# Gathered expert slots in batches of eight instead of four, and a ring of fourteen row buffers instead of twelve

## The chip, the cores and the metric

The kernel runs on one core of one Trainium2 chip. Five engines work on their own instruction streams and wait for each other by semaphores: TensorE (PE; its weight loads are PEld), VectorE (DVE), ScalarE (ACT), GpSimd (POOL) and SyncE (SP), which here only issues transfers. The metric is the time of one execution on the device in microseconds; lower is better. Where several runs are given, the median counts.

## What is computed

One layer: the input, plus attention with 32 heads of 16 columns that share one key and one value head, plus a product-key mixture of experts. 2048 tokens of 512 columns, all in fp32:

```python
xn = layernorm(x)
# A: q = xn @ wq (32 heads of 16), one k and v for all heads, softmax, @ wo
# B: for each token and each of 32 query heads
s1, s2 = q1 @ k1.T, q2 @ k2.T            # 64 scores each
i1, i2 = the two best of each            # four candidates, the two best of them: top_s, top_e
g = softmax(top_s)
act = gelu(xn . u[top_e])                # u, v: 4096 rows of 512 columns
out = sum over 32 heads x 2 of g * act * v[top_e]
return x + A(xn) + B(xn)
```

The kernel takes the 32 query heads in 8 chunks c of four. So each token has 64 expert rows: 8 chunks, four heads, two rows each.

## The kernel before

The 16 tiles of 128 tokens form four groups of four. The whole program is one long, hand-ordered stream: a start stage (layer norm, keys, values, queries), then 256 attention steps. A step is one unit of attention for one block of 128 keys: four score matmuls `sc` (L412), two exponentials `pt` on ACT (L419), sixteen matmuls `pv` (L429). Between them `fill()` lets PE do other work up to a planned time: the query-key products of the expert search (`psc`, L631) with their top-two search on DVE (L644, L646), and later the dense experts.

The experts run in two ways. For groups 0 and 1 (`NSP = 2`) each token's expert row is **gathered**. `slots` lists 512 of them: 2 groups, 8 chunks, 2 pairs of tiles, four heads, two rows a head, two tiles. A slot `m` passes through four functions, each with a counter of its own:

- `gather(m)` (L1084): POOL issues an indirect transfer (L1091) that fetches, for 128 tokens, one row of 1024 fp32 columns (u and v side by side) into a tile `g`. These tiles come from a ring of `NGB` buffers; a buffer may be written again when its last reader has run. `gathers(most)` (L1145) issues a gather only while fewer than `NGB - lent` slots lie between the next gather and the next add.
- `dot(m)` (L1096): DVE multiplies u with the normed token tile and sums (L1103, one custom operation and a read of its accumulator) into one column of a tile `act` of `SB` columns. With the last column of a batch, three small operations of `SB` columns are put on the list `CHAIN`: `gq` (L1112), `gy` (L1113) for gelu's polynomial, and `ga` (L1114), activation times gate. The gates of a chunk lie in a tile `gg` of tokens x 4 tiles x 4 heads x 2.
- `tanhs(to)` (L1162): ACT takes one tanh a batch (L1119) and marks the batch ready (`a_ready`). `weigh(n)` makes the batch's weights on DVE (L1126).
- `add(m)` (L1129): DVE adds weight times v to the tile's sum (L1138), a `scalar_tensor_tensor` of 128x512. This is the last reader of the ring buffer. The sum lies in a tile `xa`, which has the normed tokens beside it.

Groups 2 and 3 are **dense**: the gates of all tokens are spread into one-hot products (`oh` on DVE, L892 to L895; `pg` on PE, L925; the *gate stage*, `dense_on == 2`), and then 32 blocks of experts run as full matmuls `pact` (L833) and `pout` (L971), with `gy`, `wd`, `wk` and `da` on DVE in between (the *dense stage*; `wk` splits a loaded block `rw` in two parts, `gy` is the activation, `wd` the split of it).

The main loop sets the order of slots: in each step `pos` grows by a rate for the stage (1.0 dot a step in a gate stage, 1.5 in a dense stage, 1.75 to 2.6 else), and `mid()` emits, in this order, tanhs of complete batches, the step's dots but one, `weigh`, the last dot, and then `go()`: it takes adds, chain operations and operations of the other work (`rest`: `wk`, `gy`, `wd`) in turn, and at its end up to four gathers. The number of adds is at most the number of dots or three, whichever is more, and at most two once `dense_on` is 3 or 4. In a gate stage the chain runs at once, ahead of the one-hots, and `go()` later.

Three times the ring gives two of its buffers to the output weights `wo` (`lent = 2`, L484), until a block of four tiles is done. A finished tile is stored by SP (`experts_out`, L540 and L543), and the four tiles `xa` of the second group reuse the buffers of the first (`load_phase2_tile`, L1195, with the transfers L1197 and L1198), called with the first gather of each. SP issues its transfers strictly in order. `rc` (L467) is a reciprocal for the softmax sums of attention.

The lines of the batch size and the ring, as the kernel has them:

```python
SB = 4
NGB = 12
# in add(): the weight of a batch, made when its first add needs it
weigh(n)
if i == SB - 1:
    weigh(n + 1)
# in gathers():
while g_next[0] < NSL and g_next[0] < a_next[0] + NGB - lent[0] and most > 0:
# in tanhs():
while a_ready[0] + SB <= to:
    tanh(a_ready[0] // SB)
    a_ready[0] += SB
```

Of the kernel before, what the change touches and what calls it, by code (L numbers as in the profile page):

```python
# [12 lines left out]
F16 = mybir.dt.float16  # L13
# [10 lines left out]
P = 128  # L24
# [12 lines left out]
NSP = 2  # L37
NB = 32
NEG = 8
SB = 4  # L40
NGB = 12
NWK = 8
NIDX = 9
GS = 8192.0
# [14 lines left out]
def tile_kernel(ctx, tc, x, wq, wkv, wo, wqT, kT, uv, ub, vb, out):  # L59
# [3 lines left out]
    const = pool("const", bufs=1)  # L63
# [4 lines left out]
    start = start_stack.enter_context(tc.tile_pool(name="start", bufs=1))  # L68
# [44 lines left out]
    for j in range(4):  # L113
        v = blk_f[:, 8 * j:8 * j + 8]
# [4 lines left out]
    nc.gpsimd.tensor_copy(blk, blk_f)  # L119
    iota_i = start.tile([P, P], I32, name="iota_i")  # L120
    nc.gpsimd.iota(iota_i, pattern=[[1, P]], base=0, channel_multiplier=0)
    iota_h = const.tile([P, P], F16, name="iota_h")
    nc.gpsimd.tensor_copy(iota_h, iota_i)

    gtile = lambda dt=F32, shape=(P, 1024), name="g": big.tile(list(shape), dt, name=name, tag="g", bufs=NGB)
    xtile = lambda name: ps.tile([P, 512], F32, name=name, tag="x", bufs=3)
# [357 lines left out]
    def load_wo():  # L484
        WO.clear()
        for h in range(2):
            if lent[0]:
                assert g_next[0] - a_next[0] <= NGB - 2
                w = gtile(F32, (P, 2, D), "wo")
# [161 lines left out]
    IDX, G = {}, {}  # L651
# [432 lines left out]
    def gather(m):  # L1084
        ph, c, ti, s = slots[m]
        if s == 0:
            run_scores(key=(ph, c, ti))
            if ph and c == 0:
                load_phase2_tile(TPH * ph + ti)
        gt = gtile()  # L1090
        nc.gpsimd.indirect_dma_start(  # L1091
            out=gt, out_offset=None, in_=uv,
            in_offset=bass.IndirectOffsetOnAxis(ap=IDX[ph, c, ti][:, s:s + 1], axis=0))
        UV[m] = gt

    def dot(m):  # L1096
        ph, c, ti, s = slots[m]
        n, i = divmod(m, SB)
        if i == 0:
            ACTS[n] = small.tile([P, SB], F32, name="act", bufs=3)  # L1100
        a = ACTS[n]
        u = UV[m][:, :D]
        nc.vector.tensor_tensor_reduce(u, u, XN[TPH * ph + ti], scale=1.0, scalar=0.0,  # L1103
                                       op0=OP.mult, op1=OP.add, accum_out=a[:, i:i + 1])
        if i == SB - 1:
            q = small.tile([P, SB], F32, name="gq", bufs=3)
            y = small.tile([P, SB], F32, name="gy", bufs=3)
            ga = small.tile([P, SB], F32, name="ga", bufs=4)
            gg = G[ph, c][:, ti - 1:ti + 1, s // 2, :].rearrange("p t k -> p k t")
            pairs = lambda v: v.rearrange("p (k t) -> p k t", t=2)  # L1110
            stt = nc.vector.scalar_tensor_tensor
            CHAIN.append(lambda: stt(q, a, C_CUB, a, op0=OP.mult, op1=OP.mult))  # L1112
            CHAIN.append(lambda: stt(y, q, C_IN, a, op0=OP.add, op1=OP.mult))  # L1113
            CHAIN.append(lambda: nc.vector.tensor_tensor(out=pairs(ga), in0=pairs(a), in1=gg, op=OP.mult))  # L1114
            TH[n], GA[n] = y, ga
# [29 lines left out]
    def gathers(most):  # L1145
        while g_next[0] < NSL and g_next[0] < a_next[0] + NGB - lent[0] and most > 0:
            gather(g_next[0])
            g_next[0] += 1
            most -= 1

    def dots(to):
        while d_next[0] < min(to, NSL):
            dot(d_next[0])
            d_next[0] += 1
# [18 lines left out]
    def run(fns):  # L1173
        todo = fns[:]
        fns.clear()
        for fn in todo:
            fn()
# [144 lines left out]
    with tc.manual_schedule(engines=ENGINES):  # L1322
# [80 lines left out]
        load_q(0)  # L1403
        gathers(NGB // 2)
        transpose_group(3)
# [32 lines left out]
    with tc.manual_schedule(engines=ENGINES):  # L1438
# [80 lines left out]
        while a_next[0] < NSL:  # L1519
# [4 lines left out]
            run(STORES)  # L1524
            gathers(NGB)
        assert not OUTS
# [3 lines left out]
def build(nc, tc, args):  # L1530
    tile_kernel(tc, *args)
# [33 lines left out]
```

## Time and profile before

| what | value |
|---|---|
| three runs | 1822.09, 1819.43, 1818.98 us; median 1819.43 |
| the profiled execution | 1823.24 us, of which its span is 1821.5 us |
| granted TensorE clock, mean | 0.998 |
| busy, share of the span | PE 96%, DVE 89%, ACT 71%, POOL 38% |
| the chain that ended last | PE 48%, DVE 32%, DMA 6%, issue 4%, ACT 3% |

A busy microsecond is one in which the engine had an instruction under way; overlapping ones are counted once. The chain that ended last is followed back from the last instruction, at each step to what released it. In a row of the groups stand the line, the engine, the operation with the names it writes and reads, the shapes and the count; then busy microseconds in all and the mean of one in ns; then the idle time of the engine just ahead of these instructions, and who ended it. In a timeline stand start, length and the instruction, and in brackets the idle time ahead of it.

### The profile page before, as it was taken

The numbers are of one execution on the slowest core, as the hardware profiler recorded it, in microseconds if no ns is written. First come the engines' busy times: TensorE is split into PE (matmuls) and PEld (weight loads), VectorE is DVE, ScalarE is ACT, GpSimd is POOL, SyncE is SP. The second block draws the span as 40 slices with busy tenths as digits, with TensorE's granted clock in tenths as the row PEclk, the third lists the DMA queues.
The fourth block names the chain that finished last, engine by engine and source line by source line (L and its number), as shares of the span: only waits on it lengthen the run. The fifth ranks groups of instructions, "written<-read, shape, count | busy, mean of one in ns | idle before, by whom it ended". The sixth has DMA issues, their size and how long they took to land.

```text
span 1821.5 us, 34944 instructions
## 1 busy us (share of the span) xinstructions
PE 1743.2 (96%) x10997; PEld 880.0 (48%) x10997; DVE 1625.8 (89%) x6385; ACT 1290.0 (71%) x1750; POOL 698.9 (38%) x922
## 2 busy tenths in 40 slices
PE   7999999999998889999999999999988899999998
PEld 4644444555554334555555444555543344555553
DVE  7749989999899977999999798999989778999994
ACT  5367766656568987888787565556689877888874
POOL 1124544435442122444444353345521124444440
PEclk9999999999999999999999999999999999999999
DMA  8489897996764777988899987877636768898883
GB/s 287 175 303 376 303 339 248 347 336 237 242 201 132 238 243 223 284 276 290 283 313 325 321 311 240 291 249 249 229 98 232 251 189 292 286 308 286 286 283 105
DMA packets 243705, 478.31 MB, mean 263 GB/s; under 512 B 93748, under 2 KB 117316, under 8 KB 243516
## 3 DMA queue, kind: packets, MB, share of 16 engines
q0 software_dynamic: 73728, 268.47, 43.6%
q1 hardware_dynamic: 169372, 206.93, 34.2%
q8 instruction: 87, 1.43, 0.3%
q14 instruction: 102, 0.84, 0.1%
q10 hardware_dynamic: 416, 0.66, 0.1%
HBM read 419.94 MB, written 51.15 MB: 259 GB/s over the span
## 4 chain that ended last, share of the span: by engine, by line
PE 48%; DVE 32%; DMA 6%; issue 4%; ACT 3%; POOL 1%; SPq 1%; DVEq 0%; ACTq 0%; POOLq 0%
PE psc L631 16%; PE pv L429 13%; PE sc L412 8%; DVE xa L1138 7%; DVE g L1103 6%; PE pact L833 3%; DVE oh L892 3%; PE pout L971 3%; DVE i L646 2%; DVE da L974 2%; PE pwo L527 2%; ACT pt L419 2%; DVE wk L798 1%; PE pw L583 1%; DMA rsb<-dinv 1%
## 5 line engine op out<-in xcount | busy, mean ns | idle before, releaser
L419 ACT ACTIVATE pt<-sc 128x1024 f32<-128x1024 f32 x1024 | 995.9, 1030 | 379.5 <-PE sc L412 317.8
L1091 POOL DMA_INDIRECT g<-in_uv_dram,idx x512 | 561.0, 1096 | 894.7 <-DVE xa L1138 410.7
L429 PE MATMUL pv<-pt,vaug 128*32 128x512 f32 x4096 | 494.2, 600 | 0.0
L631 PE MATMUL psc<-wk,xt 128*128 128x512 f32 x1536 | 392.8, 403 | 6.9 <-DVE i L646 1.9
L1138 DVE SCALAR_TENSOR_TENSOR xa<-g,w,xa 128x512 f32<-128x512 f32 x512 | 373.5, 748 | 0.1
L412 PE MATMUL sc<-qa,kaug 64*128 64x512 f16 x2048 | 319.6, 382 | 27.6 <-ACT pt L419 22.5
L1103 DVE CUSTOM_DVE_ANT_0 g<-g,xa 128x512 f32<-128x512 f32 x512 | 336.3, 686 | 6.0 <-DMA g<-in_uv_dram,idx 5.9
L631 PEld LDWEIGHTS psc<-wk,xt 128*128 128x128 f32 x1536 | 277.2, 188 | 112.1 <-issue 42.2
L412 PEld LDWEIGHTS <-kaug 64*128 64x128 f16 x2048 | 82.4, 94 | 346.2 <-issue 341.3
L429 PEld LDWEIGHTS pv<-pt,vaug 128*32 128x32 f32 x4096 | 107.0, 109 | 254.9 <-issue 254.9
L646 DVE FIND_INDEX8 i<-m,psc 128x8 uint32<-128x64 f32 x1024 | 207.2, 227 | 0.0
L971 PE MATMUL pout<-wk,wd 128*128 128x512 f32 x768 | 195.2, 401 | 2.7 <-DVE gy L1014 1.5
L833 PE MATMUL pact<-xt,wk 128*128 128x512 f32 x768 | 196.8, 401 | 0.6 <-DVE da L974 0.6
L971 PEld LDWEIGHTS pout<-wk,wd 128*128 128x128 f32 x768 | 140.6, 188 | 49.5 <-issue 5.6
L833 PEld LDWEIGHTS pact<-xt,wk 128*128 128x128 f32 x768 | 139.3, 188 | 49.6 <-issue 18.7
L644 DVE MAX8 m<-psc 128x8 f32<-128x64 f32 x1024 | 146.5, 218 | 10.5 <-PE psc L631 10.1
L798 DVE TENSOR_TENSOR wk<-rw,wk 128x512 fp32r<-128x512 f32 x128 | 85.6, 688 | 8.1 <-ACT wk L797 8.1
L974 DVE TENSOR_TENSOR da<-da,pout 128x512 f32<-128x512 f32 x128 | 82.8, 685 | 6.2 <-PE pout L971 6.2
L892 DVE TENSOR_TENSOR oh<-oh 128x2048 f16<-128x2048 f16 x64 | 78.1, 1220 | 3.3 <-issue 1.9
L646 DVE MATCH_VALUE_LOAD i<-m,psc 128x8 f32 x1024 | 77.7, 76 | 0.0
L797 ACT CAST wk<-rw 128x512 fp32r<-128x512 f32 x128 | 74.4, 636 | 0.0
L690 POOL CAST fi<-i 128x64 f32<-128x64 uint32 x32 | 9.0, 281 | 136.7 <-DVE i L646 131.8
(179 smaller groups left out, 1341.9 us busy)
## 6 DMA issues: line engine op xcount, KB each, us to landing
wk<-dw SPq DMA_DIRECT2D x96, 512.0 KB
wqt<-in_wqT_dram SPq DMA_DIRECT2D x32, 512.0 KB
dw<-wk SPq DMA_DIRECT2D x32, 512.0 KB
rw<-in_ub_dram SPq DMA_DIRECT2D x64, 256.0 KB
rw<-in_vb_dram SPq DMA_DIRECT2D x64, 256.0 KB
gy<-dg SPq DMA_DIRECT2D x64, 256.0 KB
dg<-gst SPq DMA_DIRECT2D x14, 928.0 KB
g<-in_uv_dram,idx POOLq DMA_INDIRECT x512
```

The costliest lines, as they stand in the source:

```text
L412: nc.tensor.matmul(p[:, b, :], kaug[o:o + 64, kc * P:(kc + 1) * P], QA[u][o:o + 64, i, :], start=True, stop=True)
L419: nc.scalar.activation(PT[u, kc, i], p, AF.Exp, scale=SCALE)
L429: nc.tensor.matmul(PV[u][32 * j:32 * j + 32, :], vaug[:, kc, :], pt[:, b, :], start=kc == 0, stop=kc == 15)
L631: nc.tensor.matmul(p, XT[k][:, a, j * P:(j + 1) * P], WC[n_][k][:, bb, :], start=n == 0, stop=n == 11)
L644: nc.vector.max(m8[:, jb, s, :], p[:, s * E:(s + 1) * E])
L646: nc.vector.max_index(i8[:, jb, s, :], m8[:, jb, s, :], p[:, s * E:(s + 1) * E])
L833: nc.tensor.matmul(p, us[:, a, k * P:(k + 1) * P], XT[k][:, c, :], start=n == 0, stop=n == 11)
L892: nc.vector.tensor_tensor(out=oa, in0=num(P), in1=bc(0, tb, P), op=OP.is_equal)
L971: nc.tensor.matmul(p, wd[0][:, a, j * P:(j + 1) * P], vs[:, c, :], start=n == 0, stop=n == 5)
L1091: nc.gpsimd.indirect_dma_start(out=gt, out_offset=None, in_=uv, in_offset=bass.IndirectOffsetOnAxis(ap=IDX[ph, c, ti][:, s:s + 1], axis=0))
L1103: nc.vector.tensor_tensor_reduce(u, u, XN[TPH * ph + ti], scale=1.0, scalar=0.0, op0=OP.mult, op1=OP.add, accum_out=a[:, i:i + 1])
L1138: nc.vector.scalar_tensor_tensor(acc, v, w[:, i:i + 1], acc, op0=OP.mult, op1=OP.add)
```

## The change

`SB` goes from 4 to 8, so a batch is two heads of a pair of tiles, and there are 64 batches instead of 128. `NGB` goes from 12 to 14. To make room for the larger ring the constant `iota_h` moves to the pool that is given back after the start. The view of the gates in `dot` spans two heads instead of one.

```diff
--- before.py
+++ after.py
@@ -37,8 +37,8 @@
 NSP = 2
 NB = 32
 NEG = 8
-SB = 4
-NGB = 12
+SB = 8
+NGB = 14
 NWK = 8
 NIDX = 9
 GS = 8192.0
@@ -119,7 +119,7 @@
     nc.gpsimd.tensor_copy(blk, blk_f)
     iota_i = start.tile([P, P], I32, name="iota_i")
     nc.gpsimd.iota(iota_i, pattern=[[1, P]], base=0, channel_multiplier=0)
-    iota_h = const.tile([P, P], F16, name="iota_h")
+    iota_h = start.tile([P, P], F16, name="iota_h")
     nc.gpsimd.tensor_copy(iota_h, iota_i)
 
     gtile = lambda dt=F32, shape=(P, 1024), name="g": big.tile(list(shape), dt, name=name, tag="g", bufs=NGB)
@@ -1106,8 +1106,9 @@
             q = small.tile([P, SB], F32, name="gq", bufs=3)
             y = small.tile([P, SB], F32, name="gy", bufs=3)
             ga = small.tile([P, SB], F32, name="ga", bufs=4)
-            gg = G[ph, c][:, ti - 1:ti + 1, s // 2, :].rearrange("p t k -> p k t")
-            pairs = lambda v: v.rearrange("p (k t) -> p k t", t=2)
+            h = s // 2
+            gg = G[ph, c][:, ti - 1:ti + 1, h - 1:h + 1, :].rearrange("p t h k -> p h k t")
+            pairs = lambda v: v.rearrange("p (h k t) -> p h k t", h=2, t=2)
             stt = nc.vector.scalar_tensor_tensor
             CHAIN.append(lambda: stt(q, a, C_CUB, a, op0=OP.mult, op1=OP.mult))
             CHAIN.append(lambda: stt(y, q, C_IN, a, op0=OP.add, op1=OP.mult))
```

The instructions of PE are the same 7007 in both programs, in the same order. DVE has 3387 rows before and 3090 now (a row is one instruction as the program names it), ACT 945 and 860, POOL 419 in both, SP 842 and 840. The dots of each step are the same. The gather of a slot stands one step ahead of its dot for 33 of the 512 slots now, and for 6 before.

The first place is DVE in the first dense stage, step 121 to 122. `g` is a ring buffer (the number tells the slot's tile), `xa` a sum or a normed tile, `w` the weight of a batch, `rw`, `wk`, `gy`, `pact` belong to the dense work. Before, the last rows ahead of the dot of slot 246 (the dot of `g_11762` follows as the next row; the add that frees its buffer stands 37 rows ahead of it):

```order
L1138 SCALAR_TENSOR_TENSOR xa_162<-g_11528,w_11908,xa_162 128x512
L1112 SCALAR_TENSOR_TENSOR gq_11905<-act_11829 128x4
L798 TENSOR_TENSOR wk_11899<-rw_11722,wk_11899 128x512
L1138 SCALAR_TENSOR_TENSOR xa_164<-g_11530,w_11908,xa_164 128x512
L1113 SCALAR_TENSOR_TENSOR gy_11906<-gq_11905,act_11829 128x4
L798 TENSOR_TENSOR wk_11901<-rw_11722,wk_11901 128x512
L1138 SCALAR_TENSOR_TENSOR xa_162<-g_11532,w_11908,xa_162 128x512
L1114 TENSOR_TENSOR ga_11907<-act_11829,gg_4460 128x4
L1039 SCALAR_TENSOR_TENSOR gy_11725<-gy_11725,pact_11860 128x512
L1014 SCALAR_TENSOR_TENSOR gy_11725<-gy_11725,pact_11860 128x512
L1103 ISA g_11760,act_11910<-g_11760,xa_168 128x512
L1103 ISA act_11910 128x1
```

Now, from the add of slot 232 (`g_11066`), whose buffer slot 246 takes, to the dot of slot 246 (`g_11575`):

```order
L1139 SCALAR_TENSOR_TENSOR xa_162<-g_11066,w_11567,xa_162 128x512
L798 TENSOR_TENSOR wk_11561<-rw_11394,wk_11561 128x512
L1139 SCALAR_TENSOR_TENSOR xa_164<-g_11128,w_11567,xa_164 128x512
L798 TENSOR_TENSOR wk_11563<-rw_11394,wk_11563 128x512
L1139 SCALAR_TENSOR_TENSOR xa_162<-g_11130,w_11567,xa_162 128x512
L1039 SCALAR_TENSOR_TENSOR gy_11397<-gy_11397,pact_11522 128x512
L1014 SCALAR_TENSOR_TENSOR gy_11397<-gy_11397,pact_11522 128x512
L1103 ISA g_11427,act_11494<-g_11427,xa_168 128x512
L1103 ISA act_11494 128x1
L1103 ISA g_11575,act_11494<-g_11575,xa_166 128x512
```

The three chain operations are gone from this piece, and the add that frees the buffer has moved to nine rows ahead of the dot that needs it.

The second place is DVE in the second dense stage, around slot 405. Before, the first add frees the buffer, and the dot of slot 405 (`g_19536`) follows as the next row:

```order
L1138 SCALAR_TENSOR_TENSOR xa_12166<-g_19113,w_19453,xa_12166 128x512
L798 TENSOR_TENSOR wk_19523<-rw_19339,wk_19523 128x512
L1138 SCALAR_TENSOR_TENSOR xa_12161<-g_19161,w_19529,xa_12161 128x512
L798 TENSOR_TENSOR wk_19525<-rw_19339,wk_19525 128x512
L1138 SCALAR_TENSOR_TENSOR xa_12166<-g_19163,w_19529,xa_12166 128x512
L1039 SCALAR_TENSOR_TENSOR gy_19342<-gy_19342,pact_19491 128x512
L1014 SCALAR_TENSOR_TENSOR gy_19342<-gy_19342,pact_19491 128x512
L467 RECIPROCAL rc_19411<-rc_19411 128x32
L1103 ISA g_19469,act_19455<-g_19469,xa_12643 128x512
L1103 ISA act_19455 128x1
L1103 ISA g_19471,act_19601<-g_19471,xa_12638 128x512
L1103 ISA act_19601 128x1
```

Now, from the add that frees its buffer to its dot (`g_18983`):

```order
L1139 SCALAR_TENSOR_TENSOR xa_11875<-g_18566,w_18973,xa_11875 128x512
L798 TENSOR_TENSOR wk_18970<-rw_18792,wk_18970 128x512
L1139 SCALAR_TENSOR_TENSOR xa_11809<-g_18614,w_18973,xa_11809 128x512
L1039 SCALAR_TENSOR_TENSOR gy_18795<-gy_18795,pact_18936 128x512
L1014 SCALAR_TENSOR_TENSOR gy_18795<-gy_18795,pact_18936 128x512
L467 RECIPROCAL rc_18866<-rc_18866 128x32
L1103 ISA g_18916,act_18906<-g_18916,xa_12327 128x512
L1103 ISA act_18906 128x1
L1103 ISA g_18981,act_18906<-g_18981,xa_12264 128x512
L1103 ISA act_18906 128x1
L1103 ISA g_18983,act_18906<-g_18983,xa_12327 128x512
```

Between the freeing add and the dot there is one add and one `wk` less.

The third place is SP's queue where the tiles `xa` of the second group are loaded (steps 122 to 126); `out` is the store of a finished tile, the four `xa` rows load tiles 4 and 5. Before:

```order
L543 DMA out_0_dram<-xa_164 128x512
L764 DMA rw_12115<-in_ub_dram 128x512
L765 DMA rw_12115<-in_vb_dram 128x512
L789 DMA gy_12118<-dg_98 128x8x64
L1197 DMA xa_12161<-dxn4_84 128x512
L1198 DMA xa_12161<-in_x_dram 128x512
L1197 DMA xa_12166<-dxn5_85 128x512
L1198 DMA xa_12166<-in_x_dram 128x512
```

Now:

```order
L543 DMA out_0_dram<-xa_162 128x512
L789 DMA gy_11768<-dg_98 128x8x64
L1198 DMA xa_11809<-dxn4_84 128x512
L1199 DMA xa_11809<-in_x_dram 128x512
L764 DMA rw_11843<-in_ub_dram 128x512
L765 DMA rw_11843<-in_vb_dram 128x512
L543 DMA out_0_dram<-xa_164 128x512
L789 DMA gy_11847<-dg_98 128x8x64
L1198 DMA xa_11875<-dxn5_85 128x512
L1199 DMA xa_11875<-in_x_dram 128x512
```

The two tiles were loaded together, behind both stores. Now each follows the store whose tile it replaces, with one `gy` between, and the loads of the dense blocks `rw` stand among them.

## The prediction

> **What bounds the kernel now.** I read the stretches first, cut at the stages of the program: 119 to 319 us the last query products with the first expert slots, 319 to 563 slots beside the search (psc), 563 to 655 the first one-hot gate stage, 655 to 1010 the first dense expert stage, 1010 to 1344 slots again, 1344 to 1432 the second gate stage, 1432 to 1792 the second dense stage. Busy microseconds by engine, then clock and DMA share:
>
> ```profile
> core 0: us, PE busy (x) PEld busy (x) DVE busy (x) ACT busy (x) POOL busy (x), PEclk, DMA share, GB/s
> 119.00:319.00 200.00, 193.21 (x1155) 86.19 (x1155) 180.30 (x912) 138.16 (x186) 93.44 (x117) 1.00 0.90 316
> 319.00:563.00 244.00, 241.69 (x1428) 127.30 (x1426) 230.70 (x1470) 148.49 (x184) 117.86 (x223) 1.00 0.78 263
> 563.00:655.00 92.00, 76.24 (x953) 33.15 (x953) 89.13 (x177) 87.81 (x118) 16.99 (x15) 1.00 0.60 198
> 655.00:1010.00 355.00, 350.90 (x2028) 179.42 (x2026) 323.88 (x757) 280.91 (x397) 143.71 (x127) 1.00 0.88 286
> 1010.00:1344.00 334.00, 328.86 (x1926) 168.52 (x1922) 302.18 (x1865) 201.19 (x247) 154.33 (x265) 1.00 0.75 256
> 1344.00:1432.00 88.00, 70.96 (x911) 30.95 (x908) 86.11 (x168) 82.41 (x112) 15.94 (x14) 0.99 0.59 197
> 1432.00:1792.00 360.00, 355.68 (x2047) 180.14 (x2045) 328.94 (x777) 286.53 (x405) 142.03 (x123) 0.99 0.83 269
> ```
>
> PE (TensorE) is idle 2.3 us of the 244, 4.1 of the 355, 5.1 of the 334 and 4.3 of the 360: there the end is set by PE's own matmuls. Only in the two gate stages is it otherwise: DVE (VectorE) is busy 89.1 of 92 and 86.1 of 88, PE is idle 15.8 and 17.0. So whatever the change takes from DVE can be earned in the gate stages, perhaps in the 6.8 idle microseconds of 119 to 319, and hardly elsewhere. The costliest PE groups say it once more (the last field is idle time before them, and who ended it):
>
> ```profile
> L631 PE MATMUL psc<-wk,xt 128*128 128x512 f32 x1536 | 392.8, 403 | 6.9 <-DVE i L646 1.9 <-DMA wk<-dw 1.3 <-DVE m L644 1.1
> ...
> L971 PE MATMUL pout<-wk,wd 128*128 128x512 f32 x768 | 195.2, 401 | 2.7 <-DVE gy L1014 1.5 <-DVE wd L1034 0.8 <-DVE da L974 0.3
> ...
> L925 PE MATMUL pg<-oh 128*128 128x64 f16 (+1 forms) x1024 | 38.7, 192 | 12.0 <-DVE oh L895 11.9
> ```
>
> The search lost 3.0 us to DVE in the whole run, the second dense product 2.6, the gate matmuls 11.9.
>
> **What the change removes.** 128 batches become 64, and with each batch go three DVE operations (L1112 to L1114), the weight (L1126) and one tanh on ACT (ScalarE):
>
> ```profile
> L1112 DVE SCALAR_TENSOR_TENSOR gq<-act 128x4 f32<-128x4 f32 x128 | 20.6, 161 | 0.3
> ...
> L1126 DVE SCALAR_TENSOR_TENSOR w<-gth,ga 128x4 f32<-128x4 f32 x128 | 20.5, 160 | 40.5 <-ACT gth L1119 40.5
> ...
> L1119 ACT ACTIVATE gth<-gy 128x4 f32<-128x4 f32 x128 | 27.5, 215 | 8.1 <-DVE gy L1113 8.1
> ```
>
> By busy time that is 64 x 4 x 0.161 = 41 us of DVE and 64 x 0.215 = 13.8 us of ACT. DVE's operations overlap, though, so I price them by when the next one starts. First the chain of a gate stage in the timeline of DVE (start, length, operation):
>
> ```profile
> 594.46 0.17 DVE L1112 SCALAR_TENSOR_TENSOR gq<-act 128x4 f32<-128x4 f32 x1
> 594.66 0.16 DVE L1113 SCALAR_TENSOR_TENSOR gy<-gq,act 128x4 f32<-128x4 f32 x1
> 594.74 0.16 DVE L1114 TENSOR_TENSOR ga<-act,gg 128x4 f32<-128x4 f32 x1
> 594.81 1.22 DVE L892 TENSOR_TENSOR oh<-oh 128x2048 f16<-128x2048 f16 x1
> ```
>
> And one such operation ahead of an add, in a stretch of adds:
>
> ```profile
> 256.67 0.16 DVE L1112 SCALAR_TENSOR_TENSOR gq<-act 128x4 f32<-128x4 f32 x1
> 256.76 0.74 DVE L1138 SCALAR_TENSOR_TENSOR xa<-g,w,xa 128x512 f32<-128x512 f32 x1
> ```
>
> Back to back the three take 0.35 us; between adds one holds up the next by 0.09. So a batch costs 0.43 us of DVE's time where the chain runs at once (0.35 and 0.08 for the weight), 0.32 to 0.36 elsewhere: 64 fewer are worth 20 to 27 us of DVE, not 41, if DVE set the end everywhere. The wider operations (128x8 for 128x4) are not in the trace; between 128x4 (0.161) and the dot's 128x512 (0.686) four more columns add 4/508 x 0.525 = 0.004 us each, or nothing: I take nothing.
>
> [...]
>
> Stage by stage. In the gate stages DVE runs one dot a step, some 16 in each, so 4 batches become 2: 2 x 0.43 = 0.9 us each, 1.7 together, of which I take **-1.7** (from both sides: nothing, if the burst of adds after each batch, now 3, 3, 2 instead of 3, 1, falls in a step where PE waits anyway; -3, if the tanh's place goes as well). In 119 to 319 some 9 batches go, 3 us of DVE, beside gathers that come closer (below): **0**, from -3 to +1. In the stages of the search, where PE lost 3.0 us to DVE in all, **0**, and -1 at most. ACT is close to full in the gate stages too, 87.8 of 92 and 82.4 of 88, and PE waits for it:
>
> ```profile
> L412 PE MATMUL sc<-qa,kaug 64*128 64x512 f16 x2048 | 319.6, 382 | 27.6 <-ACT pt L419 22.5
> ```
>
> Two tanhs fewer are 0.4 us of ACT in each, at the same steps as DVE's relief and smaller, so they add nothing to it: 0.
>
> **What it adds: a shorter lead of the gathers.** A row's buffer is free for the next gather once its add has run, and an add waits for its whole batch. With 12 buffers and batches of 4, 12 - 4 = 8 rows can be on their way when a batch is complete; with 14 and 8 it is 14 - 8 = 6. In the order of the instructions this shows as 33 gathers only one step ahead of their dot, where there were 6. The trace of before has what such a closeness costs, at the start of the second dense stage (slots 405 and 408; a bracket is idle time and its releaser):
>
> ```profile
> 1504.03 0.75 DVE L1138 SCALAR_TENSOR_TENSOR xa<-g,w,xa 128x512 f32<-128x512 f32 x1
> ...
> 1505.05 1.14 POOL L1091 DMA_INDIRECT g<-in_uv_dram,idx  x1 [2.02 <-DVE xa L1138]
> ...
> 1512.78 0.69 DVE L1103 CUSTOM_DVE_ANT_0 g<-g,xa 128x512 f32<-128x512 f32 x1 [2.08 <-DMA g<-in_uv_dram,idx]
> ...
> 1513.40 0.75 DVE L1138 SCALAR_TENSOR_TENSOR xa<-g,w,xa 128x512 f32<-128x512 f32 x1
> 1514.06 0.15 DVE L1112 SCALAR_TENSOR_TENSOR gq<-act 128x4 f32<-128x4 f32 x1
> ...
> 1514.42 1.22 POOL L1091 DMA_INDIRECT g<-in_uv_dram,idx  x1 [5.05 <-DVE gq L1112]
> ...
> 1519.23 0.69 DVE L1103 CUSTOM_DVE_ANT_0 g<-g,xa 128x512 f32<-128x512 f32 x1
> ```
>
> From the end of the freeing add (1504.78) to the dot that had to wait, 8.0 us; from the next (1514.15) to a dot that didn't wait, 5.1. So a dot whose buffer is freed less than **5.1 to 8.0 us** of DVE work ahead of it may wait. What DVE waited for gathers in the whole run, and the 48 us in which it happened:
>
> ```profile
> L1103 DVE CUSTOM_DVE_ANT_0 g<-g,xa 128x512 f32<-128x512 f32 x512 | 336.3, 686 | 6.0 <-DMA g<-in_uv_dram,idx 5.9
> ```
>
> ```profile
> 1500.00:1548.00 48.00, 45.74 (x265) 22.35 (x263) 42.07 (x101) 37.53 (x54) 23.48 (x20) 1.00 0.88 287
> ```
>
> DVE is idle for 5.9 us there, which is the whole of its waiting for gathers; PE is idle for 2.3, where the other 312 us of that stage together have 2.0, or 0.3 in 48 us. So 5.9 us of waiting cost PE 2.0, and **3.9 were absorbed** by the lead that DVE has over PE. Now the first dense stage. Slot 246 was gathered long ahead; the add that freed its buffer, its gather, and DVE's rows up to its dot, the last:
>
> ```profile
> 909.53 0.75 DVE L1138 SCALAR_TENSOR_TENSOR xa<-g,w,xa 128x512 f32<-128x512 f32 x1
> ...
> 910.74 0.94 POOL L1091 DMA_INDIRECT g<-in_uv_dram,idx  x1 [0.30 <-issue]
> ...
> 923.63 0.69 DVE L1014 SCALAR_TENSOR_TENSOR gy<-gy,pact 128x512 f32<-128x512 f32 x1
> 924.23 0.70 DVE L1103 CUSTOM_DVE_ANT_0 g<-g,xa 128x512 f32<-128x512 f32 x1
> 924.84 0.10 DVE L1103 DVE_READ_ACCUMULATOR2_ANT act<- 128x1 f32 x1
> 924.84 0.70 DVE L1103 CUSTOM_DVE_ANT_0 g<-g,xa 128x512 f32<-128x512 f32 x1
> ```
>
> Its buffer was freed at 910.28, its dot ran at 924.84: 14.6 us. In the changed order (first piece shown with the change) seven operations stand between: two wk, two adds, the two gy, one dot, that is 5 x 0.60 (start to start in the rows above; wk is taken like gy) and 2 x 0.66 (the add of 1513.40, whose follower on DVE starts 0.66 later) = 4.3 us. Counted so, slots 246, 249, 254, 257, 262 and 270 have 4.2 to 5.4 us. If each needs 5.1, DVE waits some 0.4 each, 2.6 in all; if each needs up to 8.0, about 10 (a wait delays the next pair as well, so it isn't six times 3.5). I take 6, a value between, since 8.0 and 5.1 each stand in one row: less the 3.9 that DVE's lead absorbed before, PE pays **+2.1** (0 to +6.1). In the second dense stage the six dots of slots 400 to 413 have 3.7 to 5.4 us where they had 5.1 to 5.7: about one microsecond less each; a wait there has no lead left to eat, and half of them show as waits: **+2** (0 to +5). On SP's queue a store of a finished tile now stands straight ahead of the reload that waits for the same buffer (second piece of SP): it is 0 to 3 us later for dots that come two steps behind, and falls into the same waits, 0.
>
> [...]
>
> **Sum.** -1.7 + 0 + 2.1 + 2 = +2.4 us on the profiled execution, 1823.24 us (span 1821.5). That execution is 3.8 above the median of the three runs, 1819.43; the difference carried over gives **1821.8 us**. About 0.2%, 3.6 us, is what a measurement of this kernel can tell from no change; the forecast is "same".
>
> **Rivals.** (1) *Slower: the ring starves the dense stages.* The mechanism is the lead of 6 rows; it decides once the waits of a dense stage pass the 3.9 us that DVE's lead absorbs. For it: the order, and the 5.9 us that even 8 rows of lead lost. Against it: 5.1 us sufficed at 1519. With waits of 10 us in the first stage (+6.1), +5 in the second and +1 before 319, and nothing earned in the gate stages, +12.1: 1831.5; from +3.6, 1823, it counts as slower. (2) *Faster: the gathers land in time, and the relief counts.* -3 in the gate stages, -3 of the 6.8 before 319, and 12 to 14 buffers take away the 2.0 that the waits after 1504 cost: -8.0, 1811.4; with half of it, 1815.4. For it the 11.9 us that PE waits in the gate stages; against it that only four batches go there. (3) *DVE's relief counts everywhere*: -20, 1799; against it PE's idle 2 to 5 us a stage. [...] (4) *The change does not do what it says*: the wider batch shows no lost lead, since the adds come sooner than the order lets one think; then only -1.7, 1817.7, which is "same" too.
>
> **How the numbers follow.** The likeliest is the forecast with (4), 0.42. (1) has 0.37, the sum lying a microsecond from its border; (2) 0.20, (3) 0.01. So faster 0.21, same 0.42, slower 0.37. The range reaches to 1832 for (1) and to 1813 for most of (2): outside it I leave 0.05 above and 0.07 below, and some 0.06 for what I didn't see.
>
> **What would show it.** Right: the gate stages shorter by about 0.9 us each; L1103 waiting for gathers near 920 to 990 and 1500 to 1545, some 6 and 10 us in all; PE idle there rising by 2 each; the search stages unchanged to 1 us. Wrong: no DMA wait before L1103 in the first dense stage (then 2); PE idle in the search, or L1103 waits before 563 us (then 1, elsewhere); gate stages longer, if bursts of adds hold the one-hots up.

## The result and the profile after

The changed kernel takes **1840.63 us** (median of 6 runs, 1835.26 to 1841.59) against 1820.76 before (6 runs, 1818.98 to 1825.84): 1.010 times as long, 95% interval 1.0082 to 1.0118. It is slower by 1%, above the upper end of the forecast. The profiled run is the shortest of the six, 1835.26 us with a span of 1833.6, so its trace shows 12.1 of the 19.9 us. A second trace of the same kernel, on another chip, is among the experiments.

The page of the changed kernel, first its busy times, then the groups that answer to those quoted before (one added line has shifted the numbers from L1110 on by one):

```profile
span 1833.6 us, 34597 instructions
...
PE 1751.0 (95%) x10997; PEld 882.2 (48%) x10997; DVE 1608.7 (88%) x6129; ACT 1285.1 (70%) x1686; POOL 688.2 (38%) x922
...
L631 PE MATMUL psc<-wk,xt 128*128 128x512 f32 x1536 | 392.3, 403 | 2.5 <-DVE wk L593 2.2
...
L1103 DVE CUSTOM_DVE_ANT_0 g<-g,xa 128x512 f32<-128x512 f32 x512 | 335.3, 682 | 26.3 <-DMA g<-in_uv_dram,idx 21.5
...
L971 PE MATMUL pout<-wk,wd 128*128 128x512 f32 x768 | 196.5, 403 | 5.9 <-DVE gy L1014 3.1
L833 PE MATMUL pact<-xt,wk 128*128 128x512 f32 x768 | 197.0, 401 | 3.1 <-DVE da L974 3.1
```

DVE has 256 instructions fewer and 17 us less busy time, and it waits 21.5 us for gathered rows where it waited 5.9. PE is idle 82.6 us (1833.6 less 1751.0) against 78.3 before, 4.3 more. But PE is also busy 7.8 us longer, 1751.0 against 1743.2, with the same 10997 matmuls. That is the larger part of the 12.1 us, and it is not idle time.

Where the time went, by attention steps, in microseconds. A step here begins with the first of its eight `sc` matmuls in the trace: the 256 steps share 2048 `sc` and 1024 `pt`, so each holds two blocks of 128 keys, with four exponentials.

| steps | what runs | before | changed | difference |
|---|---|---|---|---|
| to 65 | start, slots beside the search | 563.0 | 561.5 | -1.5 |
| 65 to 90 | first gate stage and what follows it | 140.9 | 145.7 | +4.8 |
| 90 to 126 | first dense stage | 245.0 | 243.9 | -1.1 |
| 126 to 136 | its end, first dots on the reloaded tiles | 69.6 | 75.3 | +5.7 |
| 136 to 186 | slots beside the search | 335.3 | 332.2 | -3.1 |
| 186 to 202 | second gate stage | 86.0 | 89.9 | +3.9 |
| 202 to 208 | on to the second dense stage | 40.5 | 40.4 | -0.1 |
| 208 to 222 | start of the second dense stage | 96.4 | 100.7 | +4.3 |
| 222 to the end | | 244.7 | 244.0 | -0.7 |

Four places lose 18.7 us, the others gain 6.4. Each of the four has a wait of its own.

**First gate stage.** SP's waits between 560 and 660 us, and the rows of ACT and PE that follow (the wait of SP: line, what it waited for, total, times, longest):

```profile
SPq L494 <- DVE xa L1139: 6.1, 1, 6.1
```

```profile
594.29 1.08 SPq L494 DMA_DIRECT2D wo<-in_wo_dram  x2
595.46 0.52 SPq L935 DMA_DIRECT2D dg<-gst  x1
...
603.97 0.59 ACT L930 COPY gst<-pg 128x512 f32<-128x512 f32 x1 [2.78 <-DMA dg<-gst]
...
605.54 0.51 PE L412 MATMUL sc<-qa,kaug 64*128 64x512 f16 x2 [2.32 <-ACT pt L419]
```

`wo` borrows two buffers of the ring, so its load waits for an add; with the wider batch that add comes late, and SP waits 6.1 us for it. Before, that wait was 0.2 us (the row `SPq L494 <- DVE xa L1138: 0.2, 1, 0.2`). The stores of `gst` stand behind it on SP: the first was issued at 595.46, where before it was at 589.84. ACT needs the stored buffer and waits 2.78 us; PE waits for ACT.

**Second gate stage.** The adds of one batch on DVE, and PE just behind:

```profile
1367.02 2.07 DVE L1139 SCALAR_TENSOR_TENSOR xa<-g,w,xa 128x512 f32<-128x512 f32 x3
1373.54 2.07 DVE L1139 SCALAR_TENSOR_TENSOR xa<-g,w,xa 128x512 f32<-128x512 f32 x3
...
1378.20 0.63 PE L925 MATMUL pg<-oh 128*128 128x64 f16 x16 [0.98 <-DVE oh L895]
1380.13 0.72 PE L925 MATMUL pg<-oh 128*128 128x64 f16 x16 [1.30 <-DVE oh L895]
```

Two steps in a row have three adds each, 4.1 us ahead of the one-hots that PE waits for. Before, three adds were followed by a single one:

```profile
1362.26 2.07 DVE L1138 SCALAR_TENSOR_TENSOR xa<-g,w,xa 128x512 f32<-128x512 f32 x3
1368.72 0.75 DVE L1138 SCALAR_TENSOR_TENSOR xa<-g,w,xa 128x512 f32<-128x512 f32 x1
```

That is what the trace shows side by side; whether the bursts cost the 3.9 us is taken up with the experiments.

**End of the first dense stage.** SP's wait for the stores of the finished tiles, which stand ahead of the reload into the same buffers (915 to 962 us); then the dot that waits for a reloaded tile, and PE:

```profile
SPq L1198 <- DMA out_dram<-xa: 10.7, 2, 5.7
```

```profile
960.73 0.69 DVE L1103 CUSTOM_DVE_ANT_0 g<-g,xa 128x512 f32<-128x512 f32 x1 [4.67 <-DMA xa<-dxn]
...
966.06 1.74 PE L833 MATMUL pact<-xt,wk 128*128 128x512 f32 x6 [3.10 <-DVE da L974]
```

Before, SP waited for no store ahead of a reload, and had issued the reloads of both tiles (L1197) by 941.80; now they go out at 947.05 and 955.24.

**Start of the second dense stage.** A gathered row that comes late, and PE:

```profile
1522.97 0.69 DVE L1103 CUSTOM_DVE_ANT_0 g<-g,xa 128x512 f32<-128x512 f32 x1 [3.94 <-DMA g<-in_uv_dram,idx]
...
1527.52 2.08 PE L971 MATMUL pout<-wk,wd 128*128 128x512 f32 x4 [2.34 <-DVE gy L1014]
```

**The clock.** The longer busy time of PE goes with its clock. The trace's record of the granted clock has only the values 1.0 and 0.5, and changes them on a grid of 3.413 us: ahead of the last matmuls its stretches at half clock last 3.413 us each, in the kernel before one of 6.827. Two windows of that grid, and their neighbours, around the wait of 605.54; the seventh field is PEclk:

```profile
core 0: us, PE busy (x) PEld busy (x) DVE busy (x) ACT busy (x) POOL busy (x), PEclk, DMA share, GB/s
598.86:602.27 3.41, 2.78 (x36) 1.09 (x29) 3.34 (x6) 2.26 (x3) 0.00 (x0) 1.00 1.07 389
602.27:605.68 3.41, 0.77 (x18) 0.70 (x18) 3.38 (x7) 1.71 (x3) 0.00 (x0) 1.00 0.88 342
605.68:609.09 3.41, 3.01 (x16) 0.69 (x17) 3.38 (x7) 3.41 (x5) 0.00 (x0) 0.50 0.03 11
609.09:612.51 3.42, 2.91 (x48) 1.33 (x40) 2.96 (x6) 2.27 (x4) 0.00 (x0) 1.00 0.00 0
```

PE works 0.77 of 3.41 us, and the next window runs at half clock. The changed kernel has 8 such windows, two in the first gate stage and three in the second, one each at 967.49 and 1527.28 (the two waits above), and one at 281.41; the kernel before has 2, next to each other at the end of its second gate stage (the one behind the last matmul is left out in both). Sixteen `pv` that run wholly at half clock take 3.64 us (1433.14 in the kernel before), at full clock 1.92 (282.67 there). So six more windows of 3.41 us at half clock are, by estimate, up to 10.2 us of matmul time; 7.8 came out. PE's busy time inside its half-clock windows is 26.7 us now and 5.9 before; at full clock about half of the difference, an estimated 10.4 us, would not be there, so the windows are enough to explain the 7.8.

### The profile page after: what moved, and what is told of

Read it like the earlier page. It is cut to its first block, busy times and chain, and to the rows that moved or that the text cites. A ratio compares the mean times of both kernels' runs of the same rounds, so it can differ in the third digit from the quotient of the medians.

```text
span 1833.6 us, 34597 instructions
## 1 busy us (share of the span) xinstructions
PE 1751.0 (95%) x10997; PEld 882.2 (48%) x10997; DVE 1608.7 (88%) x6129; ACT 1285.1 (70%) x1686; POOL 688.2 (38%) x922
## 4 chain that ended last, share of the span: by engine, by line
PE 68%; DVE 10%; DMA 6%; ACT 4%; issue 4%; POOL 1%; SPq 1%; DVEq 0%; ACTq 0%; POOLq 0%
PE pv L429 19%; PE psc L631 19%; PE sc L412 11%; PE pact L833 7%; PE pout L971 7%; ACT pt L419 3%; DVE xa L1139 2%; DVE oh L892 2%; PE pwo L527 2%; DVE g L1103 1%; PE pw L583 1%; DMA dg<-gst 1%; DMA g<-in_uv_dram,idx 1%; DMA wk<-dw 1%; POOL g L1091 1%
## 5 line engine op out<-in xcount | busy, mean ns | idle before, releaser
L1091 POOL DMA_INDIRECT g<-in_uv_dram,idx x512 | 553.1, 1080 | 886.1 <-DVE xa L1139 609.1
L429 PE MATMUL pv<-pt,vaug 128*32 128x512 f32 x4096 | 500.8, 607 | 0.0
L1139 DVE SCALAR_TENSOR_TENSOR xa<-g,w,xa 128x512 f32<-128x512 f32 x512 | 368.9, 744 | 0.1
L1103 DVE CUSTOM_DVE_ANT_0 g<-g,xa 128x512 f32<-128x512 f32 x512 | 335.3, 682 | 26.3 <-DMA g<-in_uv_dram,idx 21.5
L646 DVE FIND_INDEX8 i<-m,psc 128x8 uint32<-128x64 f32 x1024 | 206.2, 219 | 0.0
L974 DVE TENSOR_TENSOR da<-da,pout 128x512 f32<-128x512 f32 x128 | 82.6, 680 | 7.2 <-PE pout L971 7.2
L646 DVE MATCH_VALUE_LOAD i<-m,psc 128x8 f32 x1024 | 69.5, 68 | 0.0
```

The lines of the kernel that those rows point to most:

```text
L429: nc.tensor.matmul(PV[u][32 * j:32 * j + 32, :], vaug[:, kc, :], pt[:, b, :], start=kc == 0, stop=kc == 15)
L646: nc.vector.max_index(i8[:, jb, s, :], m8[:, jb, s, :], p[:, s * E:(s + 1) * E])
L1091: nc.gpsimd.indirect_dma_start(out=gt, out_offset=None, in_=uv, in_offset=bass.IndirectOffsetOnAxis(ap=IDX[ph, c, ti][:, s:s + 1], axis=0))
L1139: nc.vector.scalar_tensor_tensor(acc, v, w[:, i:i + 1], acc, op0=OP.mult, op1=OP.add)
```

## The experiments

The kernel before ran beside each. A ratio is to the kernel before on the same chip, with its 95% interval. "Half-clock windows" are counted in the clock record of each profile. Waits and step times are those of one profile a kernel. Kernels with batches of eight are edits of the changed kernel, those with batches of four edits of the kernel before; `...` marks what is left out.

### One part of the change alone

```diff
 SB = 8
-NGB = 14
+NGB = 12
```

> Batches of eight with the old ring of twelve: the lead falls to 12 - 8 = 4 rows. If the loss of the change comes from the wider batch alone and the ring repays part of it, this one is slower than the changed kernel: 1850 to 1865 us, DVE's waits for gathers above the 21.5 us of the changed kernel. If the lost 19.9 us have nothing to do with the lead (gate stages, reload of xa), it stays within 4 us of the changed kernel.

2006.63 us, ratio **1.0986** (1.0968 to 1.1005). The dots' row:

```profile
L1103 DVE CUSTOM_DVE_ANT_0 g<-g,xa 128x512 f32<-128x512 f32 x512 | 342.0, 685 | 214.6 <-DMA g<-in_uv_dram,idx 209.9 <-issue 3.3 <-DVE act L1103 0.7
```

Far more than the 1850 to 1865 us that were expected: with a ring of twelve the wider batch costs ten per cent, and the two more buffers of the change repay nine tenths of it. 39 half-clock windows; PE is busy 1801.3 us with the same matmuls.

```diff
 SB = 4
-NGB = 12
+NGB = 14
-    iota_h = const.tile(...)
+    iota_h = start.tile(...)
```

> The ring of fourteen alone, batches of four (iota_h moved as in the change): the lead grows to 10 rows. If the lead decides, the 5.9 us of waits before 1548 us go and with them 2 us of PE: 1815 to 1819 us. If the larger ring costs something by itself (other places in memory, other transfers side by side), it is slower than 1821 us.

1824.02 us, ratio 1.0006 (0.9986 to 1.0027). The row of L1103 ends in `336.3, 686 | 6.0` before and `335.1, 682 | 0.0` here: all waits for rows are gone, steps 208 to 222 take 94.1 us instead of 96.4, and the whole is no faster; the 1815 to 1819 us that were expected did not come. In this profile steps 0 to 20 take 4.4 us longer than before, as they do, by 1.3 to 8 us, in 11 of the 13 other profiles of these experiments, whatever the batch; that can't be put to the change, and its cause is open.

### The same lead by another way

The prediction had counted the lead of the gathers as ring less batch: 8 before, 6 now. A ring of ten with batches of four has 6 as well.

```diff
 SB = 4
-NGB = 12
+NGB = 10
```

> The kernel before with a ring of ten: batches of four as before, but a lead of 10 - 4 = 6 rows, as in the changed kernel. If the lead alone makes the loss, DVE waits about 20 us for gathers (changed kernel 20.3 and 21.5) and the ratio is 1.008 to 1.013. If the width of the batch has its own share (adds in bursts of 3, 3, 2 and the late wo in the gate stages, some 9 us of 20), the waits are the same, but steps 65 to 90 and 186 to 202 stay within 2 us of the kernel before, and the ratio is 1.003 to 1.007.

1864.48 us, ratio **1.0222** (1.02 to 1.0245), so neither. DVE waits 44.3 us for rows, twice as long as in the changed kernel. So ring less batch does not measure the waits: with the same 6, the ring of fourteen waits 20 to 22 us and the ring of ten 44. The gate stages, on the other hand, stay near before: steps 65 to 90 take 143.2 us (140.9 before, 145.7 changed), 186 to 202 take 85.4 (86.0, 89.9). Of the excess, 18.0 us lie in steps 208 to 222.

### The loan to wo

In steps 190 to 217 two buffers of the ring are lent to `wo` (the loop below counts half steps, so its 380 is step 190). In steps 208 to 222 lie all the waits for rows of the kernel before (5.9 us), and about half of those of the changed kernel (11.3 of 21.5) and of the ring of ten (21.7 of 44.3). Both kernels were run without that loan.

```diff
-        if i in (124, 380, STEPS - 30):
+        if i in (124, STEPS - 30):
             lent[0] = 2
...
-            load_wo()
+            if i // 128 == 3 and i < STEPS - 10:
+                WO[:] = [vaug[:].rearrange("p a b -> p () (a b)").to_broadcast([P, 2, D])] * 2
+            else:
+                load_wo()
```

> The changed kernel without the second loan: the second load of wo is left out (the output projection of that block of four tiles multiplies a constant tile instead), so the ring keeps its fourteen buffers through steps 190 to 217. If the loan is what starves the rows there (14 - 2 - 8 = 4 rows of lead), DVE's waits for gathers in steps 208 to 222 go, and those steps take 94.5 to 97 us, where the changed kernel took 100.8 and 103.1; in all 4 to 8 us less than the changed kernel. If the rows are late there for another reason (the slow pace of dots before, the order of adds), the waits stay.

> The kernel before with the same left out. If the loan is the cause, its only waits for gathers (5.9 us, all between 1500 and 1548 us, with 12 - 2 - 4 = 6 rows of lead) go as well, and steps 208 to 222 take 94 to 95 us instead of 96.4; 1 to 3 us less than the kernel before, so hardly to be told from it by time alone. If not, the waits stay.

Batches of eight: 1832.17 us, ratio 1.0056 (1.0039 to 1.0073). Batches of four: 1818.02 us, ratio 0.9978 (0.9968 to 0.9988). By the ratios the first is 8 to 13 us faster than the changed kernel, where 4 to 8 were expected, and the second 4 us faster than the kernel before, where 1 to 3 were. Steps 208 to 222 in the windows of the first, then of the second:

```profile
1492.70:1586.70 94.00, 93.90 (x548) 48.29 (x547) 86.89 (x190) 76.61 (x105) 37.36 (x35) 1.00 0.86 275
```

```profile
1480.10:1574.30 94.20, 94.01 (x548) 48.33 (x549) 87.25 (x206) 76.85 (x109) 38.55 (x34) 1.00 0.83 270
```

PE is busy 93.90 of 94.00 us with batches of eight and 94.01 of 94.20 with four. Dots wait 0.3 us for rows there with batches of eight, and not at all with four. So in these steps the loan is what starves the ring: 12 - 2 - 4 = 6 rows of lead before, 14 - 2 - 8 = 4 in the changed kernel, and 10 - 2 - 4 = 4 in the ring of ten. The count tells where rows come late, not by how much: with the same 4 rows the dots of these steps wait 11.3 us in the changed kernel and 21.7 in the ring of ten.

The loan is not the whole loss. Elsewhere batches of eight still wait 9.3 us for rows without it, and by time they are 14.2 us slower than batches of four without it. Both are without one load of `wo` too, so that they are faster than their pairs is not the loan's price alone.

### The gate stages

```diff
-        ... i % 128 == (26 if i // 128 == 2 else 10) ...:
+        ... i % 128 == (26 if i // 128 == 2 else 16) ...:
             load_wo()
```

> The changed kernel with the load of wo three steps later on SP's queue, behind two stores of gst instead of ahead of them; every other engine's instructions are the same. In the changed kernel wo waited 6.1 us for an add, the stores behind it came 5.6 us later, and ACT waited 2.78 us for one of them at 603.97, PE 2.32 at 605.54, with a half-clock window right behind. If that chain is right, steps 70 to 79 take 44.7 to 46 us instead of 48.9, and the time falls by 2 to 4 us. If the burst of adds on DVE is what holds up this stage, those steps stay above 48 us.

1840.15 us, ratio 1.0087 (1.0066 to 1.0109); by time alone not to be told from the changed kernel (1.010 and, below, 1.0126). In its trace the chain is gone:

```profile
L930 ACT COPY gst<-pg 128x512 f32<-128x512 f32 x64 | 40.6, 634 | 0.0
```

ACT waits for no store of `gst` (2.8 us in the changed kernel), steps 70 to 79 take 46.4 us instead of 48.9 (44.6 before), just above what was expected, and four of the five half-clock windows of the two gate stages are gone.

The second gate stage falls too, to 84.8 us, where the changed kernel took 89.9 and the kernel before 86.0, though DVE's operations, bursts and all, are the same in the same order. So the bursts alone did not cost the 3.9 us there. Three half-clock windows have become one; SP waited for no add ahead of `wo` in that stage, so what its place on the queue changed is open. The two gate stages together take 225.5 us, less than before (226.9).

```diff
                 if dense_on[0] > 2:
                     sums = min(sums, 2)
+                elif dense_on[0] == 2:
+                    sums = min(sums, 1)
```

> The changed kernel with at most one add a step in the gate stages, so the eight adds of a batch are spread over eight steps instead of coming as 3, 3, 2. If the bursts hold up the one-hots, the second gate stage (steps 186 to 202) falls from 89.9 us to about 86 and two half-clock windows go: 2 to 4 us. If the adds merely move, it stays within 1 us there; the first gate stage may get worse, because wo waits for an add that now comes later.

1858.5 us, ratio **1.0188** (1.0174 to 1.0202): slower than the changed kernel, where 2 to 4 us less were expected. The gate stages themselves do get shorter: steps 65 to 79 take 69.1 us (75.1 changed, 70.9 before), 186 to 202 take 83.8 (89.9, 86.0). But the adds stay behind for good, and the ring starves later: DVE waits 53.9 us for rows, and steps 202 to 212 lose 11 us. A later add is a later gather. In the first gate stage SP waits for adds here as well, 2.8 and 4.5 us for the two loads of `wo`, and yet ACT waits for no store: a late `wo` by itself is not the price, only a store that comes too late behind it. Spread adds and a later `wo` each shorten these steps.

```diff
             p = xtile("pg")
+            nc.tensor.matmul(p[:, :P], ident, ident, start=True, stop=True)
```

> The changed kernel with one more matmul (128x128, fp32, about 0.28 us, result overwritten) ahead of each of the 64 groups of gate matmuls, so that PE works where it would wait. If half-clock windows come from PE doing too little in the window before, those of the gate stages go (5 in the changed kernel), at a price of up to 17.7 us of matmuls, of which some 10 lie in waits: between 3 us less and 6 us more than the changed kernel, and a mean clock of 0.995 or more. If the clock falls for another reason, the windows stay and all of the price shows.

1847.71 us, ratio 1.013 (1.0104 to 1.0155), the changed kernel on the same chip 1.0126. The clock is 0.992; four half-clock windows are left in the gate stages, where the changed kernel had five in each of its two traces. One matmul a group (`L923 PE MATMUL pg<-ident 128*128 128x128 f32 x128 | 31.0, 325 | 0.0`, so 0.48 us of PE for each of the 64) did not fill the long waits, so this run decides nothing about the clock. The time is that of the changed kernel, so the price of the matmuls (PE busy 1770.2 us, with 8 windows) lay in waits.

### The reload

```diff
-        xa = big.tile([P, 2, D], F32, name="xa", tag="xa", bufs=TPH)
-        nc.sync.dma_start(xa[:, 1, :], d_xn[t - TPH])
-        nc.sync.dma_start(xa[:, 0, :], x[t * P:(t + 1) * P, :])
-        ACC[t], XN[t] = xa[:, 0, :], xa[:, 1, :]
+        ACC[t], XN[t] = ACC[t - TPH], XN[t - TPH]
+        nc.sync.dma_start(XN[t], d_xn[t - TPH])
+        nc.sync.dma_start(ACC[t], x[t * P:(t + 1) * P, :])
```

> The changed kernel itself, beside the next three on the same chip. All theories: within 0.4% of its first measurement (ratio 1.010), a lower clock in its longer runs.

> The changed kernel with the tiles of the second group loaded into the same tile objects instead of newly allotted ones: the normed half then waits only for the old normed half's readers, and no longer for the store of the old sums; only the other half does. If the reload chain (add, store, reload, dot) is what cost steps 126 to 131 their 5.0 us, DVE's 4.67 us of wait for xa go, with PE's 3.10 and the half-clock window: 3.5 to 5 us less than the changed kernel. If the gathers alone bind there, at most 1 us.

The changed kernel again: 1848.42 us, ratio 1.0126 (1.0103 to 1.015); with xa in place: 1844.5, ratio 1.011 (1.0087 to 1.0133). That is 3.9 us less, in the range that was expected, but the intervals overlap. The traces tell more: the changed kernel, in this longer run (span 1854.8, 14 half-clock windows), waits 12.0 us for reloads and takes 84.9 us for steps 126 to 136; with xa in place that wait is gone, and they take 72.9 (69.6 before). The first row is the changed kernel's, the second the one with xa in place:

```profile
L1103 DVE CUSTOM_DVE_ANT_0 g<-g,xa 128x512 f32<-128x512 f32 x512 | 337.3, 689 | 33.3 <-DMA g<-in_uv_dram,idx 20.3 <-DMA xa<-dxn 12.0 <-issue 0.7
```

```profile
L1103 DVE CUSTOM_DVE_ANT_0 g<-g,xa 128x512 f32<-128x512 f32 x512 | 337.6, 692 | 22.5 <-DMA g<-in_uv_dram,idx 22.3
```

The waits for rows stay at 20 to 22 us: the reload is a place of its own.

### Together

The edits of the later wo and of xa in place, in one kernel; then the same with at most two adds a step in the gate stages.

> The changed kernel with both: wo three steps later, and xa in place. If the three places are separate, the gains add: 6 to 9 us less than the changed kernel, 1831 to 1834 on the scale of the first measurement; what is left above the kernel before would be the gathers of steps 212 to 217 (4.7 us) and bursts of adds in the second gate stage. If waits only move to the next scarce place, less than 4.

1837.74 us, ratio **1.007** (1.0046 to 1.0094), 10.7 us less than the changed kernel beside it; the intervals (1.0103 to 1.015 there) don't overlap. 6 to 9 us were expected. 5 half-clock windows, three of them in the first gate stage: steps 65 to 79 take 74.9 us here, though neither SP nor ACT waits as in the changed kernel, so the chain behind `wo` is not all of the loss there.

> The changed kernel with wo later, xa in place and at most two adds a step in the gate stages (2, 2, 2, 2 for 3, 3, 2). Against the run with wo and xa alone (ratio 1.007): if the bursts matter, 1 to 3 us less; if the later adds cost as much in rows that come late as they save, the same or up to 4 us more.

1836.09 us, ratio 1.0058 (1.0039 to 1.0077), not to be told from the one before it by time. Its gate stages, though, are the shortest with batches of eight:

```profile
569.10:709.30 140.20, 123.57 (x1201) 52.93 (x1202) 119.97 (x234) 122.59 (x161) 31.80 (x28) 0.99 0.66 215
1358.30:1441.10 82.80, 67.67 (x845) 30.07 (x842) 79.45 (x151) 78.81 (x105) 17.97 (x14) 1.00 0.65 216
```

140.2 and 82.8 us, where the kernel before took 140.9 and 86.0 and the changed one 145.7 and 89.9. This profile is the shortest of seven runs, 4.8 us over before in its span. In it steps 212 to 217 are 4.8 us over, the place of the loan, and steps 0 to 20 are 5.8 over. No run joins these edits with a ring that lends nothing.

### A version with batches of four

> Batches of four, ring of fourteen, xa in place: the lead of 10 rows (no wait for gathers in the run with the ring alone) and no reload wait. If waits for rows and reloads are all that can be had, 2 to 5 us less than the kernel before; if the ring's gain is eaten elsewhere again, as in the run with the ring alone (ratio 1.0006), no difference.

> As the one before, and at most one add a step in the gate stages, so batches of four come as 1, 1, 1, 1 instead of 3, 1. With a lead of 10 rows the late adds should not starve the ring as they did with batches of eight. If bursts of adds hold up the one-hots, the two gate stages (before: 71 us in steps 65 to 79, 86 in 186 to 202) get 2 to 5 us shorter in all, and a half-clock window or two go; if not, the same as the one before.

1822.5 us, ratio 0.999 (0.9975 to 1.0005), and 1822.29, ratio 0.9987 (0.9973 to 1.0001). Neither can be told from the kernel before. The first one's profile is the shortest span of all (1814.5 us), with one half-clock window and PE busy 1740.5 us, but the other runs of it are longer. The cap did nothing for the second: its gate stages take 140.2 and 86.0 us, those of the first 140.0 and 84.2.

## Why the prediction was wrong

**The bounds.** Right for the search and the dense stages: DVE is busy 17 us less and ACT 4.9 (1285.1 against 1290.0), and it earned nothing there. Steps 136 to 186 are 3.1 us shorter, but not by the change: steps 136 to 150, 96.0 us in the one profile of before, take 92.7 to 94.8 in 13 of the 15 others, batches of four among them.

**Gate stages, -1.7.** The step that failed first. They cost +8.7 (+9.2 in the second trace), outside the bounds of 0 and -3: 4.8 us of it is PE idle, 3.9 PE busy for longer. The prediction had the bursts 3, 3, 2 in its bounds, as "nothing", and took the stage for one where only DVE's sum of work counts. It missed that two buffers of the ring go to `wo` in the middle of it, and that SP's load waits for an add with the stores of `gst` behind it; the order of SP was read only around the reload. In the one trace with nothing but `wo` moved the loss is gone in both stages, in the second for a reason that is open; with xa in place as well, the first stage (steps 65 to 90) is 1.9 us above before. With wo later and the adds spread, the stages are 0.7 and 3.2 us shorter than before, but that a relief of the forecast size is behind it is not shown: batches of four scatter by as much, from 83.6 to 86.0 us in the second stage, and from 140.0 to 145.3 in steps 65 to 90, the longest of them with three half-clock windows there.

**First dense stage, +2.1 by gathers.** +5.7 in steps 126 to 136, but from another cause: the reload of xa, costed at 0 as something that "falls into the same waits". It waited 4.67 and 12.0 us by itself. Without it these steps are 3.3 us above before; but batches of four with a ring of fourteen, where no dot waits for a row, are 2.5 above as well, so what the gathers cost here is not shown. That +5.7 lies within the term's bounds (0 to +6.1) is luck.

**Second dense stage, +2.** The right place and cause, inside the bounds (0 to +5) and too small: +4.3 (+6.6 in the second trace). DVE waits 11.3 us for rows in these steps, about the 10 that were named, 8.1 of them from 1518 to 1533. A wait of 3.94 in one piece is not absorbed: PE lost 2.34 at 1527.52 and had a half-clock window behind it, an estimated 1.6. The reason why the waits lie there at all, the loan, was overlooked, though `lent` was described; the lead at that place is 6 and 4 rows, not 8 and 6.

**The clock, not in the sum.** Nothing in the prediction had PE's own matmuls get slower. 7.8 of 12.1 us are that. The row of 1344 to 1432 and the next in its first table show 0.99 for before, and were read past. The windows of that kernel at half clock lie from 1430.52 to 1437.35 us, across the border of the two rows. What stood ahead of such windows in the traces is in the last section.

**The rivals.** The first, slower by starved rows in the dense stages, was the true direction, at 0.37. Its mechanism is shown, as one part of the loss: with more rows the waits go, with fewer they grow, and without the loan 14.2 us between the two batch sizes remain. That its +12.1 equals the difference of the two profiles is luck: the gate stages, the reload and the clock were not in it. By the medians it was 19.9. The second, by which the gathers land in time, is refuted by 21.5 us of waits for rows, where before there were 5.9. Of the signs of being wrong that were named, rows that come late before 563 us are there too, 3.2 us of waits, but that stretch is no longer than before.

**Still open.** The share of the clock was not taken away by an experiment: the matmuls put into the waits did not suffice. It rests on the same matmuls being busy longer with more windows: take away half of PE's busy time inside its half-clock windows, and 14 of the 15 traces with the same matmuls have 1737.5 to 1741.0 us left, before and changed among them (the one with 39 windows 1744.8). Since the half-clock windows stand behind waits (last section), the two shares are better read as one loss. Open also are the second gate stage and the 14.2 us that batches of eight lose without the loan, where the trace still has ACT's wait for a store of `gst` (2.5 us), DVE's for reloads (5.6) and for rows (9.6), but not what each costs.

## What to carry to other kernels

A wider batch holds buffers longer: here the waits for rows went from 5.9 to 21.5 us. Count the rows that can be on their way, the ring less the batch less whatever else borrows from the ring, at the place where most is lent; here it told where rows come late (steps 208 to 222), though not by how much (11.3 and 21.7 us with the same 4 rows). Look too at each transfer behind the borrower on an in-order queue (the first store of `gst` behind `wo` went out at 595.46 us, before at 589.84). Before a saving on one engine is booked, look which transfers wait for the buffers that it now gives back later. And in this kernel a wait that left PE working less than 40% of a 3.41 us window was followed by a window at half clock each time (66 of 66), an estimated 1.6 us of matmul time.

## What the runs showed of the hardware

Over the 16 traces here, cut on the clock's own grid (30 to 1790 us; PE's busy time from the merged spans of its matmuls; windows at full clock):

| PE busy in a window | windows | next one at half clock |
|---|---|---|
| under 0.4 | 66 | 66 |
| 0.4 to 0.5 | 41 | 27 |
| 0.5 to 0.6 | 95 | 18 |
| 0.6 to 0.7 | 207 | 3 |
| 0.7 and more | 7698 | 0 |

PE at work for less than 40% of a window was followed by half clock each time (66 of 66), the window with 0.77 of 3.41 us above among them. Between 40 and 60% both happened (45 of 136). In the kernel before, two windows with nearly the same PE work, 1.56 and 1.61 of 3.41 us, went differently:

```profile
276.81:280.23 3.42, 1.56 (x8) 0.95 (x6) 3.42 (x24) 1.14 (x2) 2.81 (x3) 1.00 0.39 107
280.23:283.64 3.41, 2.77 (x23) 1.36 (x27) 2.57 (x10) 1.58 (x3) 0.33 (x1) 1.00 0.94 291
```

```profile
1427.11:1430.52 3.41, 1.61 (x29) 1.01 (x29) 3.34 (x7) 3.41 (x6) 1.21 (x2) 1.00 0.95 316
1430.52:1433.93 3.41, 2.48 (x21) 0.91 (x21) 2.86 (x9) 3.41 (x6) 1.15 (x1) 0.50 0.67 201
```

The windows lie differently against the work in the traces of the two kernels. A wait of PE for DVE's search (`i`, L646), 2.50 us up to 280.87 in the kernel before, is shared by the first two windows shown here, and no half clock follows; in the changed kernel it is 2.29 us up to 280.56 and falls into the one window from 278.00 to 281.41, in which PE works 1.12 us, and the next runs at half clock. That this makes part of the spread of the runs is likely, not shown; in 23 runs of the kernel before on one chip the shortest, 1817.61 us, has a mean clock of 0.998 and the longest, 1831.75, one of 0.990.

The price of a window follows from the kernels with the same 10997 matmuls: PE is busy 1740.5 us with 1 half-clock window (batches of four, xa in place), 1743.2 with 2 (before), 1751.0 with 8 (changed), 1757.8 with 14 (changed again), 1801.3 with 39 (batches of eight, ring of twelve): (1801.3 - 1740.5) / 38 = 1.6 us each, an estimate, close to half of 3.41.
